# Sliding-window attention and an ELU feed-forward layer: two phases rewritten as one stream with a written-out order

## The chip, the cores and the metric

The kernel runs on one core of one Trainium2 chip. A core has a matrix engine (PE, with its weight loads listed apart as PEld), a vector engine (DVE), an activation engine (ACT), a general-purpose engine (POOL) that also issues transfers, and a sync engine (SP) that only issues transfers; 16 DMA engines move the data. Each engine works through its own list of instructions in order and waits on semaphores. The metric is the device time of one execution in microseconds (us). The kernel before takes 479.98 us, the median of two runs (479.75 to 480.21).

## The reference

Queries, keys and values are [8 batches, 8 heads, 576 positions, 64], all in 32-bit floats. Every query sees the keys at most 32 positions away. The attention output, brought to 4608 tokens by 512, goes through a feed-forward layer (FFN) of width 2048 with an ELU between its two products.

```python
scores = scale * np.matmul(q, k.transpose(0, 1, 3, 2))
mask = np.abs(pos[:, None] - pos[None, :]) <= window      # window = 32
scores = np.where(mask, scores, -1000000000.0)
attn = softmax(scores)
x = (attn @ v).transpose(0, 2, 1, 3).reshape(4608, 512)
h = x @ w_in                                              # 512 -> 2048
g = np.where(h > 0.0, h, np.exp(np.minimum(h, 0.0)) - 1.0)
out = g @ w_out                                           # 2048 -> 512
```

## The kernel before

The program has three stages, one behind the other.

**Attention**, by batch and in it by query block of 64 positions (nine per batch). POOL loads q and k (line 133) and v (lines 167 to 175) from 32-bit to 16-bit on the way, in rows of 64 elements; v is loaded twice, in two tiles shifted by 32 and 96 rows, so that every 128-row key window begins at a tile's row 0. PE turns q and k over, five 128x128 transposes for two heads at a time (line 148), and DVE and ACT take turns in copying the result out (lines 152, 154). For a query block PE makes scores for eight heads against a window of 128 keys (line 188, a contraction of 64), ACT takes the exponential (line 197), DVE multiplies by the 0/1 mask (line 200), and PE makes per head one product with v (line 209) and one with a column of ones (line 212), which is the softmax's denominator. ACT copies the product out (line 218), DVE takes the reciprocal (line 222) and scales (line 225) into `x_st`. There are 72 query blocks.

**Turning x over**: 36 chunks of 128 tokens, four transposes each (line 237), copied by DVE (line 240) and ACT (line 242) in turn.

**FFN**: 18 tiles of 256 tokens. Each has four groups of four 128-wide slices of the hidden layer: 16 matmuls of 256 columns into `psH` (line 263), one exponential over 1024 elements (line 269), two DVE steps for the ELU (`f_sb`, line 271, and `g_sb`, line 273), then eight matmuls of 512 columns into `psY` (line 278). After four groups ACT copies `psY` out (line 285) and SP stores it.

The program is written in this order; a scheduler decides, by dependence and by free buffers, where each instruction stands on its engine, so attention of the next batch is drawn between that of this one. Loads of the two weights (lines 228, 230) stand on POOL behind all loads of q, k and v. The pools of the attention stage are closed before the FFN's are opened, and the FFN's first matmul reads `xT` after the turning-over stage:

```python
    with tc.tile_pool(name="attn_stg", bufs=2) as spool, \
    ...
    with tc.tile_pool(name="xtr_ps", bufs=4, space=bass.MemoryType.PSUM) as xps_pool:
    ...
    with tc.tile_pool(name="moe_sb", bufs=3) as mpool, \
```

## Time and profile before

| what | value |
|---|---|
| time, median of two runs | 479.98 us |
| span of the profiled execution | 479.4 us |
| attention, from its first score matmul to the first transpose of x | 18.4 to 188.1 us |
| turning x over | 188.1 to 200.4 us |
| FFN, first to last matmul | 200.4 to 474.3 us |
| busy share PE / DVE / ACT / POOL | 84% / 53% / 42% / 28% |

The profiled execution is one run; its span, from the first to the last instruction, is 0.6 us below the median time, so what is worked out against the span is compared with the time by adding that. A matmul's duration in the profile holds its way through the array: consecutive ones overlap, so the pace is read from a run of them (the last start to the first, over their number), not from the mean. "Idle before" is the time that the engine waited just before a group, and what ended it. PEclk is the clock that was granted to TensorE as a share of full speed.

### The profile page before, as it was taken

The page shows a single profiled execution, that of the slowest core. Times are in us where ns is not written, and L with a number is a line of the kernel's source. Part 1 is how long each engine was busy: PE and PEld are TensorE (multiplying, and loading weights), DVE is VectorE, ACT ScalarE, POOL GpSimd, SP SyncE. Part 2 cuts the span into 40 slices and gives each one's busy share as a digit, 9 for nine tenths or more (in the row PEclk, how much of TensorE's full clock was granted, in tenths as well). Part 3 has the DMA queues.
Part 4 walks back from the last instruction along what each step waited for, and adds up shares of the span by engine and source line. Part 5 has one row for each costly group of instructions (what it writes and reads, how often), then busy time and mean ns, then how long its engine had stood idle before and what let it go on. Part 6 is the DMA issues. An engine that isn't in the chain of part 4 may idle for free.

```text
span 479.4 us, 9261 instructions
## 1 busy us (share of the span) xinstructions
PE 402.1 (84%) x3889; PEld 282.6 (59%) x3920; DVE 252.2 (53%) x474; ACT 203.5 (42%) x285; POOL 135.8 (28%) x227
## 2 busy tenths in 40 slices
PE   1676877777687876999999999999999999999994
PEld 0465766656575756856565565656656565665652
DVE  0364757567574756564554635445364554635443
ACT  1364656556574655723242333423334143332422
POOL 9999989979777000000000000000000000000000
PEclk9999999999555555999999999999999999999998
DMA  9999999999999990001110111101111011100111
GB/s 61 121 134 152 129 117 153 132 103 153 88 142 92 207 165 1 2 1 44 45 45 0 46 44 45 45 0 45 44 46 40 5 45 44 45 22 24 45 44 44
DMA packets 157033, 33.10 MB, mean 69 GB/s; under 512 B 149824, under 2 KB 151872, under 8 KB 156992
## 3 DMA queue, kind: packets, MB, share of 16 engines
q0 software_dynamic: 152096, 23.08, 70.0%
q1 hardware_dynamic: 4896, 9.44, 5.1%
q8 instruction: 30, 0.49, 0.5%
q14 instruction: 11, 0.09, 0.1%
HBM read 46.14 MB, written 9.44 MB: 116 GB/s over the span
## 4 chain that ended last, share of the span: by engine, by line
PE 46%; DVE 24%; ACT 16%; issue 7%; POOL 3%; DMA 2%; DVEq 0%; ACTq 0%; POOLq 0%
PE psY L278 28%; DVE g_sb L273 9%; ACT e_sb L269 8%; DVE x_st L225 7%; DVE f_sb L271 5%; PE psO L209 5%; PE pt L148 5%; PE psS L212 4%; ACT tT L154 3%; ACT pu L197 2%; PE psH L263 2%; PE psS L188 2%; DVE pm L200 2%; DMA vt<-in_v_dram 2%; ACT xT L242 1%
## 5 line engine op out<-in xcount | busy, mean ns | idle before, releaser
L278 PE MATMUL psY<-w_out_sb,g_sb 128*128 128x512 bf16 x545 | 134.5, 380 | 15.8 <-DVE g_sb L273 14.0
L263 PE MATMUL psH<-xT,w_in_sb 128*128 128x256 bf16 x1152 | 137.4, 273 | 0.7 <-ACT xT L242 0.7
L263 PEld LDWEIGHTS <-w_in_sb 128*128 128x128 bf16 x1152 | 112.7, 98 | 25.0 <-issue 0.8
L269 ACT ACTIVATE e_sb<-psH 128x1024 f32<-128x1024 f32 x72 | 73.8, 1026 | 108.5 <-PE psH L263 95.5
L271 DVE TENSOR_SCALAR f_sb<-e_sb 128x1024 bf16<-128x1024 f32 x72 | 49.5, 688 | 130.3 <-ACT e_sb L269 130.3
L278 PEld LDWEIGHTS <-g_sb 128*128 128x128 bf16 x576 | 50.4, 98 | 86.1 <-DVE g_sb L273 35.1
L273 DVE SCALAR_TENSOR_TENSOR g_sb<-psH,f_sb 128x1024 bf16<-128x1024 f32 x72 | 88.2, 1224 | 7.5
L209 PE MATMUL psO<-vt,pm 128*64 128x64 bf16 x576 | 48.3, 241 | 18.6 <-DVE pm L200 17.2
L209 PEld LDWEIGHTS <-pm 128*64 128x64 bf16 x576 | 41.2, 152 | 25.8 <-DVE pm L200 20.8
L212 PE MATMUL psS<-ones_col,pm 128*64 128x1 bf16 x576 | 45.7, 193 | 9.4 <-ACT pu L197 6.3
L218 ACT COPY oc<-psO 64x512 f32<-64x512 f32 x72 | 41.7, 580 | 27.2 <-PE psS L212 19.0
L197 ACT ACTIVATE pu<-psS 128x512 bf16<-128x512 f32 x72 | 39.5, 594 | 29.3 <-PE psS L188 29.1
L225 DVE TENSOR_TENSOR x_st<-oc,rc_t 64x512 bf16<-64x512 f32 x72 | 49.4, 686 | 4.1 <-ACT oc L218 1.5
L285 ACT COPY y_sb<-psY 128x1024 f32<-128x1024 f32 x18 | 18.2, 1012 | 76.1 <-PE psY L278 76.1
L212 PEld LDWEIGHTS <-pm 128*64 128x64 bf16 x576 | 42.7, 153 | 11.8 <-DVE pm L200 11.8
L200 DVE TENSOR_TENSOR pm<-pu,masks 128x512 bf16<-128x512 bf16 x72 | 29.1, 422 | 31.1 <-ACT pu L197 21.1
L133 POOL DMA_DIRECT2D k_ph<-in_k_dram x40 | 33.9, 868 | 7.2 <-DMA vt<-in_v_dram 6.7
L133 POOL DMA_DIRECT2D q_ph<-in_q_dram x40 | 34.1, 872 | 0.1
L154 ACT COPY tT<-pt 128x640 bf16<-128x640 bf16 x32 | 22.2, 693 | 27.7 <-PE pt L148 27.2
L148 PE MATMUL pt<-ident,q_ph 128*128 128x128 bf16 x160 | 24.7, 300 | 10.7 <-DMA q_ph<-in_q_dram 9.7
L148 PE MATMUL pt<-ident,k_ph 128*128 128x128 bf16 x160 | 21.5, 307 | 13.3 <-ACT tT L154 8.9
L169 POOL DMA_DIRECT2D vt<-in_v_dram x16 | 30.6, 1915 | 0.3 <-issue 0.3
(33 smaller groups left out, 190.4 us busy)
## 6 DMA issues: line engine op xcount, KB each, us to landing
out_dram<-y_sb SPq DMA_DIRECT2D x18, 512.0 KB, 2.8
vt<-in_v_dram POOLq DMA_DIRECT2D x16, 560.0 KB, 8.5
q_ph<-in_q_dram POOLq DMA_DIRECT2D x32, 128.0 KB, 7.4
k_ph<-in_k_dram POOLq DMA_DIRECT2D x32, 128.0 KB, 5.7
w_in_sb<-in_moe_w_in_dram POOLq DMA_DIRECT2D x1, 2048.0 KB, 16.2
w_out_sb<-in_moe_w_out_dram POOLq DMA_DIRECT2D x1, 2048.0 KB, 25.6
q_ph<-in_q_dram POOLq DMA_DIRECT2D x8, 64.0 KB, 7.3
k_ph<-in_k_dram POOLq DMA_DIRECT2D x8, 64.0 KB, 4.5
```

The costliest lines, as they stand in the source:

```text
L133: nc.gpsimd.dma_start(out=dst[0:np_, so, :, :], in_=src_hbm[b, :, lo:hi, :].rearrange("h p d -> p h d"))
L148: nc.tensor.transpose(pt[:, so, :], src[:, so, 2 * hp:2 * hp + 2, :], ident)
L197: nc.scalar.activation(pu, psS_hq, AX.Exp, scale=SCALE)
L209: nc.tensor.matmul(psO[bq:bq + QB, h, :], lhsT=pm[:, h, :], rhs=vt[:, c, :], start=True, stop=True)
L212: nc.tensor.matmul(psS[bq:bq + QB, h % 2, (h // 2) * QB:(h // 2) * QB + 1], lhsT=pm[:, h, :], rhs=ones_col, start=True, stop=True)
L218: nc.scalar.copy(oc[bq:bq + QB], psO[bq:bq + QB])
L225: nc.vector.tensor_mul(x_st[bq:bq + QB, chk, :], oc[bq:bq + QB], rcb)
L263: nc.tensor.matmul(psH[:, j, :], lhsT=w_in_sb[:, do, fo * 128:(fo + 1) * 128], rhs=xT[:, do, tok0:tok0 + TT], start=(do == 0), stop=(do == ...
L269: nc.scalar.activation(e_sb, psH, AX.Exp)
L271: nc.vector.tensor_scalar(f_sb, e_sb, -1.0, 0.0, ALU.add, ALU.min)
L273: nc.vector.scalar_tensor_tensor(g_sb, psH, 0.0, f_sb, ALU.max, ALU.add)
L278: nc.tensor.matmul(psY[:, ts, :], lhsT=g_sb[:, j, ts * 128:(ts + 1) * 128], rhs=w_out_sb[:, fo, :], start=(fg == 0 and j == 0), stop=(fg = ...
```

## The change

The three stages become one program whose instructions are put on the engines in the order in which they are written (`tc.manual_schedule()`).

Attention is cut into pieces for a pair of query blocks (36 pairs of 128 tokens): `QK` (16 score matmuls) with `SM` (one exponential over 1024 elements), `MK` (two mask multiplies of 512 elements) with `AV` for heads 0 to 3, `AV` for heads 4 to 7, and `X` (four transposes and a copy by DVE). The masked weights lie in a tile with 64 zero columns behind each block's 64 (`pm`, three times 64 wide per head), so that the two blocks' products with v, each with 128 weight columns, add up in one PSUM tile of 128 tokens; v has a 65th column of ones, so the denominator comes with the product (eight matmuls of 65 columns for four heads). `T` turns over q or k for two heads: six transposes of 96 columns and a copy by ACT. The FFN tile is 512 tokens: `Hm` is four matmuls of 512 columns and an exponential over 512 elements, `Hv` the two DVE steps, `Y` four matmuls of 512 columns.

q and k are loaded by SP without a change of type, in rows of 384 elements that lie together in memory; the cast to 16 bit is done on the chip, for batch 0 by DVE and ACT, for the others by POOL. v is loaded once, for the even query blocks; the odd blocks' windows are copied from those within the on-chip memory by SP (`shift_v`). The weights are loaded in eight parts by POOL, behind v of batch 0 and ahead of v of batch 1.

Work of pairs is divided into steps; step i holds `QK` and `SM` of pair i, `MK` and `AV` of pair i-1, `X` of pair i-2. Steps 0 to 5 are emitted before the first `Hm`. After that FFN tile t gives 16 slots of `Hm` for tile t and, from the second tile on, 16 of `Y` for tile t-1, and the remaining attention pieces are laid between the slots. `Hv` of a slot is emitted behind the next slot. PSUM holds one buffer each for scores (two banks), attention output, transposes and `Y`, and three for `Hm`.

```diff
+    def load_qk(b, half, eng):
+        for nm, src in (("q", q), ("k", k)):
+            t = stg.tile([PR, HP, TPP * D], FP32, tag="stg")
+            eng.dma_start(
+                out=t, in_=src[b, half * HP:(half + 1) * HP].rearrange(
+                    "h (p t) d -> p h (t d)", t=TPP))
...
+    def load_v(b):
+        vt = vw[b % NVB]
+        vb = v[b].rearrange("h s d -> s h d")
+        nc.gpsimd.dma_start(out=vt[WIN:128, 0, :, 0:D], in_=vb[0:128 - WIN])
+        for qb in range(2, NQB - 1, 2):
+            lo = qb * QB - WIN
+            nc.gpsimd.dma_start(out=vt[:, qb, :, 0:D], in_=vb[lo:lo + 128])
...
+    def shift_v(b):
+        vt = vw[b % NVB]
+        nc.sync.dma_start(out=vt[0:QB, 1:NQB:2], in_=vt[QB:128, 0:NQB - 1:2])
+        nc.sync.dma_start(out=vt[QB:128, 1:NQB:2], in_=vt[0:QB, 2:NQB:2])
+
+    def T(b, nm, hp):
+        src = stage[nm, b]
+        pt = psT_p.tile([128, TPP, PR], BF16, tag="psT")
+        for j in range(TPP):
+            nc.tensor.transpose(pt[:, j, :], src[:, j, 2 * hp:2 * hp + 2, :],
+                                ident[0:PR, 0:PR])
...
+        nc.scalar.copy(dst.rearrange("c (p t) -> c t p", t=TPP), pt)
...
+    def QK(i):
+        psS = psS_p.tile([128, 2, 2, HP, QB], FP32, tag="psS")
+        for s in range(2):
...
+                nc.tensor.matmul(
+                    psS[:, h % 2, s, hp, :],
...
+    def SM(i):
...
+        nc.scalar.activation(pu, psS, AX.Exp, scale=SCALE)
...
+    def MK(i):
...
+            nc.vector.tensor_mul(dst, pu[:, :, s], mb)
+
+    def AV(i, g):
...
+                nc.tensor.matmul(
+                    o[:, j, :], lhsT=p[:, h, s * QB:s * QB + 128],
+                    rhs=vw[b % NVB][:, qb, h, :],
+                    start=(s == 0), stop=(s == 1))
+        rc = xsp.tile([128, HP], FP32, tag="rc")
+        nc.vector.reciprocal(rc, o[:, :, D])
+        rb = _bap(rc, [rc.ap[0], rc.ap[1], [0, D]])
+        nc.vector.tensor_mul(live["X", i][:, g * HP:(g + 1) * HP, :],
+                             o[:, :, 0:D], rb)
...
+    def Hm(t, fo):
...
+        ps = psH_p.tile([128, TT], FP32, tag="psH")
+        for do in range(NDO):
+            nc.tensor.matmul(ps, lhsT=w_in_sb[:, do, fo * 128:(fo + 1) * 128],
+                             rhs=xts[t][:, do, :],
+                             start=(do == 0), stop=(do == NDO - 1))
+        e = ep.tile([128, TT], FP32, tag="e")
+        nc.scalar.activation(e, ps, AX.Exp)
+        es[t, fo] = (ps, e)
+
+    def Hv(t, fo):
+        ps, e = es.pop((t, fo))
+        f = ep.tile([128, TT], BF16, tag="f")
+        nc.vector.tensor_scalar(f, e, -1.0, 0.0, ALU.add, ALU.min)
+        nc.vector.tensor_tensor(gs[t][:, fo, :], ps, f, ALU.max)
...
+        for b in range(1, B):
+            need = (b * NQB) // 2
+            extra[max(0, need - 6)].append(
+                lambda b=b: (load_v(b), load_qk(b, 0, nc.sync),
+                             load_qk(b, 1, nc.sync)))
+            extra[max(0, need - 5)].append(
+                lambda b=b: (cast(b, "q", (nc.gpsimd, nc.gpsimd)),
+                             cast(b, "k", (nc.gpsimd, nc.gpsimd)),
+                             shift_v(b)))
+            for hp in range(HP):
+                extra[need - 4 + hp].append(lambda b=b, hp=hp: T(b, "q", hp))
+                extra[need - 4 + hp].append(lambda b=b, hp=hp: T(b, "k", hp))
...
+            for n, (f, a, s) in enumerate(slots):
+                f(a, s)
+                if waiting is not None:
+                    Hv(*waiting)
+                    waiting = None
+                if f is Hm:
+                    waiting = (a, s)
+                want = base + (goal - base) * (n + 1) // max(1, len(slots) - 2)
+                while pos < min(want, goal):
+                    rest[pos][1]()
+                    pos += 1
```

How this moves instructions is shown at two places. The first is DVE. In the kernel before, in the middle of the attention stage, DVE's list holds attention only (`pm` is the mask multiply, `rc_t` the reciprocal, `x_st` the scaled output, `tT` a copy of turned-over q or k):

```order
L225 TENSOR_TENSOR x_st_86<-oc_1628,rc_t_1630 64x512
L225 TENSOR_TENSOR x_st_86<-oc_1663,rc_t_1665 64x512
L200 TENSOR_TENSOR pm_1679<-pu_1677,masks_75 128x512
L200 TENSOR_TENSOR pm_1714<-pu_1712,masks_75 128x512
L152 COPY tT_1787<-pt_1789 128x640
L222 RECIPROCAL rc_t_1700<-psS_1668 64x8
L222 RECIPROCAL rc_t_1735<-psS_1703 64x8
L225 TENSOR_TENSOR x_st_86<-oc_1698,rc_t_1700 64x512
```

Every mask multiply there stands behind other attention work. In the changed kernel, in the third FFN tile, the same engine's list is this (`f` and `g` are the two steps of `Hv`, `pm0` the masked weights, `o` the product with v, `xt` the turned-over x):

```order
L216 TENSOR_SCALAR f_2043<-e_2028 128x512
L217 TENSOR_TENSOR g_1605<-ps_2023,f_2043 128x512
L165 TENSOR_TENSOR pm0_108<-pu_1870,masks_98 128x2x4x64 x2
L181 RECIPROCAL rc_2058<-o_2049 128x4
L183 TENSOR_TENSOR xs_2048<-o_2049,rc_2058 128x256
L216 TENSOR_SCALAR f_2080<-e_2066 128x512
L217 TENSOR_TENSOR g_1605<-ps_2061,f_2080 128x512
L181 RECIPROCAL rc_2092<-o_2083 128x4
L183 TENSOR_TENSOR xs_2048<-o_2083,rc_2092 128x256
L216 TENSOR_SCALAR f_2114<-e_2100 128x512
L217 TENSOR_TENSOR g_1605<-ps_2095,f_2114 128x512
L197 COPY xt_1718<-pt_2117 128x4x128
```

The two mask multiplies now stand behind `f` and `g` of an `Hm` slot, and `f` waits for that slot's exponential.

The second place is POOL. In the kernel before its list ends with the last batch's v and the two weights:

```order
L167 DMA vt_3110<-in_v_dram 96x64
L169 DMA vt_3110<-in_v_dram 128x35x64
L175 DMA vt_3110<-in_v_dram 32x64
L162 MEMSET vt_3118 32x64 x3
L165 MEMSET vt_3118 32x64
L167 DMA vt_3118<-in_v_dram 32x64
L169 DMA vt_3118<-in_v_dram 128x35x64
L175 DMA vt_3118<-in_v_dram 96x64
L228 DMA w_in_sb_80<-in_moe_w_in_dram 128x4x2048
L230 DMA w_out_sb_81<-in_moe_w_out_dram 128x16x512
```

In the changed kernel the weights stand near the front of POOL's list, between v of batch 0 (`vw0`) and v of batch 1 (`vw1`), and the casts of batch 1's q (`t_267`) and k (`t_270`) follow:

```order
L109 DMA vw0_105<-in_v_dram 96x8x64
L112 DMA vw0_105<-in_v_dram 128x8x64 x3
L114 DMA vw0_105<-in_v_dram 96x8x64
L276 DMA w_in_sb_99<-in_moe_w_in_dram 128x4x512 x4
L280 DMA w_out_sb_100<-in_moe_w_out_dram 128x4x512 x4
L109 DMA vw1_106<-in_v_dram 96x8x64
L112 DMA vw1_106<-in_v_dram 128x8x64 x3
L114 DMA vw1_106<-in_v_dram 96x8x64
L103 CAST t_267<-t_259 96x4x6x64
L103 CAST t_267<-t_263 96x4x6x64
L103 CAST t_270<-t_261 96x4x6x64
L103 CAST t_270<-t_265 96x4x6x64
```

The weights moved from the end of the list to near its front, and casts, which POOL did not have before but for the mask, came in. On SP, which before issued only the 18 stores, `shift_v` of batch 0 now stands ahead of the loads of batch 1's q and k, and waits for v of batch 0 to land.

More of the change, by code (lines that the diff above doesn't have):

```diff
@@ L13 @@
 ALU = mybir.AluOpType
+PSUM = bass.MemoryType.PSUM
 def _bap(ap, new_ap):
@@ L53 @@
     N_TOK = B * S
-    D_MODEL = H * D
+    DM = H * D
     D_FF = moe_w_in.shape[1]
@@ new lines @@
+    psH_p = ctx.enter_context(tc.tile_pool(name="psH", bufs=3, space=PSUM))
+    psY_p = ctx.enter_context(tc.tile_pool(name="psY", bufs=1, space=PSUM))
+    ident = const.tile([128, 128], BF16)
+    masks = const.tile([128, 3, QB], BF16)
+    w_in_sb = const.tile([128, NDO, D_FF], BF16)
+    w_out_sb = const.tile([128, NFO, DM], BF16)
+    NKB = 2
+    NVB = 3
+    NPB = 2
+    kT = [const.tile([128, HP, KW], BF16, name=f"kT{i}") for i in range(NKB)]
+    qT = [const.tile([128, HP, S], BF16, name=f"qT{i}") for i in range(NKB)]
@@ new lines, in cast @@
+    def cast(b, nm, engs):
+        t = bfp.tile([PR, TPP, H, D], BF16, tag="bf")
+        for half in range(2):
+            src = stage.pop((nm, b, half)).rearrange(
+                "p h (t d) -> p h t d", t=TPP)
+            dst = t[:, :, half * HP:(half + 1) * HP, :].rearrange(
+                "p t h d -> p h t d")
+            e = engs[half]
+            if e is nc.scalar:
+                nc.scalar.copy(dst, src)
+            else:
+                e.tensor_copy(dst, src)
+        stage[nm, b] = t
```

385 lines of the change are left out of this document (169 added, 216 removed).

## The prediction

> **What bounds the kernel now.** I read the page's busy shares and slices first, then the windows by stage, then the chain and the timeline inside the FFN.
>
> ```profile
> PE 402.1 (84%) x3889; PEld 282.6 (59%) x3920; DVE 252.2 (53%) x474; ACT 203.5 (42%) x285; POOL 135.8 (28%) x227
> PEclk9999999999555555999999999999999999999998
> ...
> 18.40:188.10 169.70, 126.34 (x2009) 104.95 (x2009) 106.61 (x292) 99.72 (x173) 118.57 (x186) 0.80 1.86 130
> 188.10:200.40 12.30, 11.64 (x144) 11.03 (x144) 8.33 (x19) 10.16 (x19) 0.00 (x0) 0.78 0.00 1
> 200.40:474.30 273.90, 257.97 (x1697) 163.04 (x1727) 134.69 (x144) 89.30 (x89) 0.00 (x0) 1.00 0.09 33
> ```
>
> The window rows give, behind the length, busy time of PE, PEld, DVE, ACT and POOL, then the granted clock. There are two different limits. The FFN takes 273.9 us at clock 1.00 with PE busy 94%. Attention takes 169.7 us with no engine busy more than 74%: scores, exponential, mask and product wait for each other in turn. PE's 84% is thus a mean of a full stage and one that holds many short matmuls. What the FFN must cost on PE:
>
> ```profile
> 300.45 3.22 PE L263 MATMUL psH<-xT,w_in_sb 128*128 128x256 bf16 x28
> 300.87 1.02 ACT L269 ACTIVATE e_sb<-psH 128x1024 f32<-128x1024 f32 x1 [4.82 <-PE psH L263]
> 301.92 0.69 DVE L271 TENSOR_SCALAR f_sb<-e_sb 128x1024 bf16<-128x1024 f32 x1 [3.27 <-ACT e_sb L269]
> 302.72 1.23 DVE L273 SCALAR_TENSOR_TENSOR g_sb<-psH,f_sb 128x1024 bf16<-128x1024 f32 x1
> 304.00 1.90 PE L278 MATMUL psY<-w_out_sb,g_sb 128*128 128x512 bf16 x8 [0.33 <-DVE g_sb L273]
> L278 PE MATMUL psY<-w_out_sb,g_sb 128*128 128x512 bf16 x545 | 134.5, 380 | 15.8 <-DVE g_sb L273 14.0
> ```
>
> Eight 512-column matmuls take 1.90 us of which the last's own length is 0.38: seven starts in 1.52, 0.217 us each. The whole FFN is 1152 times that (half of it now cut in 256s), 250 us; 24 of the 273.9 are waits. So most of what can go is the 200 us before the FFN, if its PE work fits beside 250 us of FFN.
>
> **The PE work of the change.** The big matmuls stay at 1152 x 0.217 = 250 us. The small ones:
>
> ```profile
> 61.69 1.23 PE L148 MATMUL pt<-ident,k_ph 128*128 128x128 bf16 x10 [0.94 <-DVE tT L152]
> 66.09 0.77 PE L188 MATMUL psS<-tT 64*128 64x64 bf16 x16
> L188 PE MATMUL psS<-tT 64*128 64x64 bf16 x576 | 26.4, 235 | 3.3 <-ACT tT L154 2.8 <-DVE rc_t L222 0.5
> L148 PE MATMUL pt<-ident,q_ph 128*128 128x128 bf16 x160 | 24.7, 300 | 10.7 <-DMA q_ph<-in_q_dram 9.7
> 193.46 6.93 ACT L242 COPY xT<-psXT 128x512 bf16<-128x512 bf16 x13 [0.27 <-PE psXT L237]
> 196.00:197.00 1.00, 1.00 (x19) 0.79 (x3) 1.00 (x3) 1.00 0.00 0
> ```
>
> Scores: 16 in 0.77, less 0.24 of the last, over fifteen, so 0.036 each and 0.58 per pair. A transpose with 128 weight columns in the attention stage: 10 in 1.23, less 0.30 of the last, over nine, gives 0.103. At granted clock 1.00 (the fourth number behind the window's length in the last row), from 193.46 on, ACT makes 13 copies in 6.93 us without a pause, each with its neighbour on DVE standing for eight transposes: 0.067 each, and there ACT sets the pace, so PE needs no more. The new stream runs like the FFN, at clock 1.00, so I take 0.060 for every matmul with 128 weight columns (`AV` 576, `T` 384, `X` 144), with 0.052 (half of 0.103, the pace following the clock) and 0.103 as ends. The Trainium skill, "TensorE: Matmul & The Clock Gate", section LDWEIGHTS, gives a weight load as its columns over 1.2 GHz, 107 ns for 128; by that the sum would be some 42 us longer. The warm stretch above speaks against it: 67 ns.
>
> Of these, 18 `T`, 6 `QK`, ten half `AV` and 4 `X` are done before the first `Hm`. What is left after it: 900 x 0.060 = 54, 480 scores x 0.036 = 17, big 250: **321 us** (314 to 360). Gone are the second product with ones (576), the second shifted v and 72 copies on ACT (line 218).
>
> **Until the first `Hm`.**
>
> ```profile
> q1 hardware_dynamic: 4896, 9.44, 5.1%
> out_dram<-y_sb SPq DMA_DIRECT2D x18, 512.0 KB, 2.8
> 168.00:172.00 4.00, 1.95 (x26) 1.43 (x25) 1.55 (x4) 2.35 (x4) 0.00 (x0) 0.50 1.24 208
> 3.70 1.00 POOL L133 DMA_DIRECT2D q_ph<-in_q_dram  x1
> 7.25 0.13 PEld L148 LDWEIGHTS <-q_ph 128*128 128x128 bf16 x2 [7.25 <-DMA q_ph<-in_q_dram]
> L133 POOL DMA_DIRECT2D k_ph<-in_k_dram x40 | 33.9, 868 | 7.2 <-DMA vt<-in_v_dram 6.7
> L93 POOL CAST masks<-mask_f 128x192 bf16<-128x192 f32 x1 | 0.4, 361 | 0.0
> L77 POOL MEMSET mask_f<- 128x192 f32 x1 | 0.3, 259 | 0.0
> L128 POOL MEMSET q_ph<- 64x512 bf16 x8 | 4.2, 524 | 0.3
> L154 ACT COPY tT<-pt 128x640 bf16<-128x640 bf16 x32 | 22.2, 693 | 27.7 <-PE pt L148 27.2
> L197 ACT ACTIVATE pu<-psS 128x512 bf16<-128x512 f32 x72 | 39.5, 594 | 29.3 <-PE psS L188 29.1
> L200 DVE TENSOR_TENSOR pm<-pu,masks 128x512 bf16<-128x512 bf16 x72 | 29.1, 422 | 31.1 <-ACT pu L197 21.1
> L222 DVE RECIPROCAL rc_t<-psS 64x8 f32<-64x8 f32 x72 | 14.8, 205 | 23.1 <-PE psS L212 22.6
> L225 DVE TENSOR_TENSOR x_st<-oc,rc_t 64x512 bf16<-64x512 f32 x72 | 49.4, 686 | 4.1 <-ACT oc L218 1.5
> L240 DVE COPY xT<-psXT 128x512 bf16<-128x512 bf16 x18 | 7.6, 424 | 3.1 <-PE psXT L237 2.0
> ```
>
> SP's stores moved 9.44 MB in 5.1% of 16 engines' 479.4 us, 24.4 us, so 386 GB/s while they ran. Batch 0's q and k, 2.36 MB in 32 bits, need 6.1 us; with 2.8 to land and the casts (1536 elements, by L269's 1.02 us for 1024 about 1.5 on ACT, two in a row) they are ready at 13. Eight `T` then follow one by one, as one transpose buffer must be emptied by ACT each time: PE 0.62 and 0.2 for the last one's way out, the copy 576/640 of 693 ns, hand-overs 0.1: 1.5 each, done at 25.
>
> Batch 1 is later. POOL starts its first load at 3.70; five loads of v at 868 ns bring it to 8, and v lands about 4 later (3.6 us pass from the first issue at 3.70 to the first transpose at 7.25). Only then does SP, held by `shift_v`, issue batch 1's q and k, at 12.5. They share the engines with the weights, 4.2 MB at the 208 GB/s of the last stretch in which only weights move, 20 us; at half their rate they take 12 and are all in at 26. POOL's casts of 1536 elements: the two memsets, 259 ns for 192 elements and 524 for 512, give 0.83 ns an element, so 361 + 1344 x 0.83 = 1.5 us; in proportion to the 192-element cast it would be 2.9. I take 2.2, and with two casts done before the last load is in, the fourth ends at 31. Step 0's second `T` needs it. Five steps follow; a step there goes round DVE and the one output buffer: product's end 0.2, reciprocal 0.2, hand-over 0.1, scaling 0.44 (256 elements, between 205 and 686 ns), `X` copy 0.42, two masks 0.84 (L200), eight `AV` matmuls at the cold 0.103 = 0.82, scaling again 0.8, and `AV` 0.82, 0.2 of hand-overs: 4.9. So 31 + 24.5, and two `T` of batch 2 at its end: **57 us** (46 if batch 1's data come as soon as batch 0's turn is over; 68 if the weights hold up v of batch 1 and a cast takes 2.9).
>
> **Waits of PE in the stream.** Order decides: PE's `AV` needs both masks, which on DVE stand behind `f` and `g` of a slot. From the last big matmul's start slot: 0.16 way out and 0.04, exponential 0.59 (L197, same size), 0.03, `f` 0.42 (half of L271's 0.69, plus the fixed part), 0.11, `g` 0.60 (512 elements as L225, 0.69, the next op starting 0.09 before its end), masks 2 x 0.42, 0.05: 2.84 us. `AV`'s eight matmuls end seven starts later, 2.84 + 0.42, where without a wait they would end 0.48 after arrival; so the wait is 2.78 less the PE work between that `Hm` and `AV`. In the order of the 27 pairs from the second tile on, this is `T Y` ten times (1.23, wait 1.55), `Y` six times (0.87, wait 1.91), `QK Y` once (1.33), `Y T Hm` twice (0.68), `QK Y Hm` three times (0.46), `QK Y T Hm` four times (0.10), `Y Hm` once (1.04): 33 us. In the first tile, without `Y`, DVE is the longer: 16 x (0.42 + 0.11 + 0.60) + 4 x 2.74 (a pair's masks 0.84, two reciprocals with scalings 1.48, `X` copy 0.42) = 29 us against PE's 24, and it waits some 0.7 for each first product: 8 us. The last tile's `Y` run alone, and three times the one `Y` buffer must be copied out (0.85): 3; the second half of a pair waits for its buffer now and then: 1. Together **45 us** (25 if slots overlap better; 75).
>
> **The casts against DVE.** Four casts of 2.2 per batch fall into the stream for six batches. The trace has no POOL compute beside DVE but memsets, under which L200 stays at 422 ns, so the bounds are nothing and all of 24 x 2.2 = 53 us. I take one mask multiply per batch held for half a cast: **7 us**. The Trainium skill, "SBUF — State Buffer", section "SBUF: two separate sides", says that a DVE instruction in a two-port mode or with two inputs in SBUF and a POOL instruction that reads SBUF exclude each other, the later one fully blocked; no run here shows it. If each cast held PE for its whole length by that, the sum would be 482.
>
> **Sum.** After the last `Y`: way out 0.2, copy 0.6, then as before 4.0 from the copy's end to the span's:
>
> ```profile
> 474.33 1.01 ACT L285 COPY y_sb<-psY 128x1024 f32<-128x1024 f32 x1 [4.23 <-PE psY L278]
> ```
>
> (475.34 to 479.4.) 57 + 321 + 45 + 7 + 5 = 435 us of span, and 0.6 between span and median: **436 us**, 9% less. ACT (144 x 0.59 + 36 x 1.03 + 64 x 0.62 + 36 x 0.59 = 183) and DVE (144 x 1.13 + 36 x 2.74 = 261) stay below that. The transfers of a batch, 2.36 MB at 386 GB/s and 0.59 MB of v at the 130 GB/s of the attention row, take 11 of the 48 us that 4.5 steps last; stores that queue on SP behind `shift_v` and behind loads have three buffers and one store in 10 us.
>
> **Rivals.**
> 1. *POOL comes late, slower than before.* `T` of the last-cast half of k follows its load by two steps, about 21 us at 10.6 a step; load 8 and four casts must fit in 22. Up to 3.4 us a cast nothing is late. At 5.8 (twice 2.9, by waiting for DVE) each of six batches stops PE for 9, and the start grows by 14: 504. From 5.2 on it passes the time before. For it: POOL's price is known from 192 elements only; against: 0.83 ns per element.
> 2. *The casts hold DVE.* Each of the 24 keeps `f` or a mask waiting for half its length to all of it, and PE with them: 26 to 53 us in place of 7, so 455 to 482. For it: both then read the same memory at once; against: PE may run three `Hm` ahead of DVE, 5 us, so a late `f` alone costs nothing.
> 3. *The small matmuls keep the cold pace.* For: attention ran at 0.103 also where the clock is given as 1.00; against: the 13 copies. 900 x 0.043 = 39 more: 475.
> 4. *A longer start*: v of batch 1 waits for all weights, 20 us, and steps wait for it: 452.
> 5. *Few waits*: the masks are mostly in time: 435 - 33 - 7, about 396.
>
> **Chances.** Forecast 0.58, longer start 0.10, few waits 0.08, cold pace 0.08 (spread around 475, half under 470), casts that hold DVE 0.08 (half under 470), POOL late 0.08. A change of 2% (470.4 to 489.6) is what a measurement here tells from none. Faster 0.84, same 0.08, slower 0.08. The terms' ends together give 390 to 560, but they won't all fall on one side: 404 to 458 for the forecast itself, and 402 to 474 leaves out most of rivals 5 and 1 and the far ends of 2 and 3, under 0.2.
>
> **What would show it.** First `Hm` near 57 us, with `T` before it waiting for a POOL cast; `AV` groups led by an idle of 1.5 us ended by the mask multiply, some 30 us in all; transposes in the stream at 0.06 per start with granted clock 1.00; `T` never waiting for POOL after the first tile. It is wrong if the clock falls in the stream, if the casts last over 3.4 us, or if the big matmuls start further apart than 0.217.

## The result, and the profile after

The changed kernel takes 453.31 us (451.61 and 455.0) against 479.98: a ratio of 0.945, with a 95% interval of 0.936 to 0.954. It is faster by 5.5%, not by the 9% of the forecast; the profiled execution's span is 449.9 us against the 435 of the sum. (Of the runs below, one of e5_serial took 661.95 us at a granted clock of 0.80; its times are those of its three other runs.) Two lines of the page, then the windows by stage (length, busy time of PE, PEld, DVE, ACT and POOL, granted clock, DMA share, GB/s):

```profile
PE 337.4 (75%) x2784; PEld 173.8 (39%) x2832; DVE 261.9 (58%) x557; ACT 268.3 (60%) x283; POOL 84.9 (19%) x92
...
PEclk9999999999989999969999999999899999999999
```

```profile
0.00:78.40 78.40, 22.42 (x300) 17.98 (x301) 22.24 (x51) 46.72 (x27) 36.19 (x51) 1.00 1.54 207
...
112.00:382.00 270.00, 230.94 (x1933) 115.66 (x1968) 180.51 (x385) 172.03 (x194) 36.97 (x31) 0.97 0.36 75
382.00:429.00 47.00, 45.84 (x243) 21.31 (x246) 32.62 (x66) 19.37 (x33) 0.00 (x0) 1.00 0.09 34
```

The first `Hm` starts at 78.4 us instead of the forecast 57. PE's share fell from 84% to 75%, and the kernel is faster all the same: PE has less to do (337 us in place of 402). Where attention runs beside the FFN, from 112 to 382 us, PE idles 39 of 270 us and the mean clock is 0.97; without attention, from 382 on, it idles 1 of 47.

What PE and its weight loads waited for from the first `Hm` on (sum in us, times, longest):

```profile
PEld L176 <- DVE pm L165: 53.9, 62, 3.4
PE o L176 <- DVE pm L165: 33.2, 25, 2.9
...
PE pt L195 <- ACT kT L131: 6.0, 10, 1.3
...
PE pt L125 <- ACT qT L131: 1.6, 3, 0.6
```

The waits for the mask product (`pm`, line 165) lead by far. They show twice: on PE's matmuls after the idle of the array, 33.2 us, and on the weight load ahead of them, 53.9, part of which lies under matmuls that still run. The time that they cost should lie between.

The groups of instructions that came out otherwise than priced (busy us, mean ns of one):

```profile
L131 ACT COPY kT<-pt 128x576 bf16<-128x576 bf16 x32 | 66.7, 2084 | 12.0 <-PE pt L125 11.5
L103 POOL CAST t<-t 96x1536 bf16<-96x1536 f32 x28 | 41.8, 1522 | 130.8 <-DMA t<-in_q_dram 130.6 <-DMA t<-in_k_dram 0.2
L216 DVE TENSOR_SCALAR f<-e 128x512 bf16<-128x512 f32 x144 | 71.3, 495 | 78.2 <-ACT e L210 78.0
L165 DVE TENSOR_TENSOR pm<-pu,masks 128x512 bf16<-128x512 bf16 x72 | 34.7, 523 | 29.0 <-ACT pu L153 29.0
```

ACT's copy of the transposed q or k lasts 2.08 us, not the 0.62 taken from the kernel before; there are 64 such copies. The POOL cast lasts 1.52 us, not 2.2. `f` and the mask take 495 and 523 ns on the mean where the forecast had 420 for each.

One stretch shows how these meet. First PE, then DVE and POOL at the same place, then the window row of what follows:

```profile
187.61 1.03 PE L227 MATMUL psY<-w_out_sb,g 128*128 128x512 bf16 x4
191.51 0.23 PE L176 MATMUL o<-vw,pm 128*128 128x65 bf16 x1 [2.87 <-DVE pm L165]
193.11 0.57 PE L176 MATMUL o<-vw,pm 128*128 128x65 bf16 x7 [1.37 <-DVE pm L165]
193.49 1.90 PE L206 MATMUL ps<-xt,w_in_sb 128*128 128x512 bf16 x4
...
203.80 1.04 PE L206 MATMUL ps<-xt,w_in_sb 128*128 128x512 bf16 x4
204.67 0.42 PE L125 MATMUL pt<-ident,t 96*128 96x96 bf16 x6
204.93 1.03 PE L227 MATMUL psY<-w_out_sb,g 128*128 128x512 bf16 x4
```

```profile
188.28 1.58 DVE L216 TENSOR_SCALAR f<-e 128x512 bf16<-128x512 f32 x1 [1.11 <-ACT e L210]
...
190.50 2.56 DVE L165 TENSOR_TENSOR pm<-pu,masks 128x512 bf16<-128x512 bf16 x2
...
188.11 4.67 POOL L103 CAST t<-t 96x1536 bf16<-96x1536 f32 x3 [3.79 <-DMA t<-in_q_dram]
...
191.30:198.10 6.80, 5.22 (x31) 2.76 (x32) 3.53 (x7) 2.58 (x2) 3.97 (x4) 0.50 0.93 76
```

While POOL casts, `f` lasts 1.58 us and two masks 2.56, and `AV` waits twice, 4.2 us in all. Then the granted clock is 0.50 for 6.8 us: four matmuls of `Hm` take 1.90 us where they take 1.04 at full clock. So a long wait is paid twice, as idle time and as slow matmuls behind it.

### The profile page after: what moved, and what is told of

Read it like the earlier page. It is cut to its first block, busy times and chain, and to the rows that moved or that the text cites. A ratio compares the mean times of both kernels' runs of the same rounds, so it can differ in the third digit from the quotient of the medians.

```text
span 449.9 us, 7032 instructions
## 1 busy us (share of the span) xinstructions
PE 337.4 (75%) x2784; PEld 173.8 (39%) x2832; DVE 261.9 (58%) x557; ACT 268.3 (60%) x283; POOL 84.9 (19%) x92
## 4 chain that ended last, share of the span: by engine, by line
PE 49%; DVE 17%; ACT 13%; DMA 13%; issue 6%; POOL 1%; SPq 0%; ACTq 0%; POOLq 0%
PE ps L206 20%; PE psY L227 20%; DMA vw<-in_v_dram 6%; DVE g L217 6%; ACT kT L131 5%; DVE f L216 5%; DVE pm L165 5%; DMA w_out_sb<-in_moe_w_out_dram 5%; ACT e L210 5%; PE o L176 4%; DMA t<-in_q_dram 2%; PE pt L125 2%; PE pt L195 2%; ACT qT L131 2%; ACT pu L153 1%
## 5 line engine op out<-in xcount | busy, mean ns | idle before, releaser
L210 ACT ACTIVATE e<-ps 128x512 f32<-128x512 f32 x144 | 92.1, 640 | 113.4 <-PE ps L206 105.6
L206 PE MATMUL ps<-xt,w_in_sb 128*128 128x512 bf16 x549 | 148.6, 389 | 2.8 <-DVE xt L197 1.3
L227 PE MATMUL psY<-w_out_sb,g 128*128 128x512 bf16 x555 | 144.7, 382 | 5.6 <-ACT y L232 3.6
L216 DVE TENSOR_SCALAR f<-e 128x512 bf16<-128x512 f32 x144 | 71.3, 495 | 78.2 <-ACT e L210 78.0
L217 DVE TENSOR_TENSOR g<-ps,f 128x512 bf16<-128x512 f32 x144 | 99.6, 692 | 5.4
L227 PEld LDWEIGHTS <-g 128*128 128x128 bf16 x576 | 52.8, 99 | 58.8 <-issue 6.7
L131 ACT COPY kT<-pt 128x576 bf16<-128x576 bf16 x32 | 66.7, 2084 | 12.0 <-PE pt L125 11.5
L206 PEld LDWEIGHTS <-w_in_sb 128*128 128x128 bf16 x576 | 51.4, 99 | 49.8 <-issue 5.2
L131 ACT COPY qT<-pt 128x576 bf16<-128x576 bf16 x32 | 66.6, 2082 | 5.0 <-PE pt L125 4.7
L103 POOL CAST t<-t 96x1536 bf16<-96x1536 f32 x28 | 41.8, 1522 | 130.8 <-DMA t<-in_q_dram 130.6
L125 PEld LDWEIGHTS <-t 96*128 96x128 bf16 x384 | 26.9, 110 | 63.6 <-issue 35.3
```

What stands on the lines that cost most here:

```text
L103: e.tensor_copy(dst, src)
L125: nc.tensor.transpose(pt[:, j, :], src[:, j, 2 * hp:2 * hp + 2, :], ident[0:PR, 0:PR])
L131: nc.scalar.copy(dst.rearrange("c (p t) -> c t p", t=TPP), pt)
L206: nc.tensor.matmul(ps, lhsT=w_in_sb[:, do, fo * 128:(fo + 1) * 128], rhs=xts[t][:, do, :], start=(do == 0), stop=(do == NDO - 1))
L210: nc.scalar.activation(e, ps, AX.Exp)
L216: nc.vector.tensor_scalar(f, e, -1.0, 0.0, ALU.add, ALU.min)
```

## The experiments

All times are medians; each ratio is to the kernel before, run beside it. The table takes five readings from one profile of each kernel: the start of the first `Hm`, the rest of the span after it, in that rest the waits of `AV`'s weight load for masks, the time at half clock (granted clock over windows of 1 us, up to 4 us before the end), and the cold time. This last is the stretch from the first `Hm` to the trace's first record of the clock: the rows read 1.00 there, but the matmuls run at the half pace (in e1_copy four matmuls of `Hm` take 1.90 us at 84.79, and three take 0.81 at 87.60). Runs of one kernel differ by up to 5.7 us (e1_copy, 438.55 to 444.29), so differences of a few us between two profiles show little.

| kernel | us | ratio, interval | first Hm | rest | mask waits | half clock | cold |
|---|---|---|---|---|---|---|---|
| after | 453.3 | 0.945, 0.936 to 0.954 | 78.4 | 371.5 | 53.9 | 17.1 | 3.6 |
| e1_copy | 441.7 | 0.922, 0.917 to 0.927 | 78.1 | 361.2 | 55.2 | 10.2 | 9.2 |
| e2_order | 466.0 | 0.973, 0.969 to 0.977 | 77.4 | 388.6 | 58.1 | 30.7 | 4.2 |
| e3_dmacast | 439.8 | 0.919, 0.915 to 0.923 | 77.6 | 360.2 | 47.4 | 3.4 | 6.0 |
| e4_mkearly | 414.6 | 0.868, 0.863 to 0.873 | 79.2 | 333.7 | 3.5 | 0 | 4.8 |
| e5_serial | 536.5 | 1.118, 1.114 to 1.122 | 275.8 | 260.5 | - | 0 | 4.3 |
| e6_order2 | 456.4 | 0.951, 0.947 to 0.954 | 77.1 | 376.5 | 54.8 | 23.9 | 8.9 |
| e7_copy_order | 432.4 | 0.901, 0.897 to 0.905 | 63.6 | 365.6 | 50.7 | 23.9 | 5.6 |
| e8_all | 384.8 | 0.802, 0.799 to 0.804 | 61.6 | 322.4 | 9.6 | 6.8 | 3.2 |
| e9_act | 424.9 | 0.884, 0.879 to 0.889 | 87.2 | 332.3 | 8.1 | 10.2 | 4.1 |
| e10_dve | 420.2 | 0.874, 0.871 to 0.877 | 90.5 | 329.4 | 4.0 | 6.8 | 4.9 |
| e11_mix | 410.7 | 0.855, 0.853 to 0.857 | 89.5 | 320.0 | 4.9 | 0 | 3.8 |
| e12_mix | 380.1 | 0.792, 0.789 to 0.794 | 58.6 | 320.0 | 4.3 | 3.4 | 5.4 |

In e9_act to e11_mix some products read another batch's v (see there). The questions were four: what holds the start, what the slow copies cost, what the casts on POOL cost, and what the place of the mask product costs. The start first. The chain of waits of after, cut to its steps:

```profile
15.99 21.35 DMA w_out_sb<-in_moe_w_out_dram
...
37.63 16.70 DMA vw<-in_v_dram
...
54.35 0.60 SPq L119
...
55.04 10.86 DMA t<-in_q_dram
...
73.00 1.48 POOL t L103
...
74.52 0.68 PE pt L125 x6
```

v of batch 1 waits for the weights on POOL's queue; SP's copy within `vw` (line 119, `shift_v`) waits for that v; batch 2's q stands behind it on SP; then come the casts and `T`. Theory A is that this chain sets the start; rival B, that the 16 slow copies do.

### e1_copy: the copy writes contiguously

```diff
-        nc.scalar.copy(dst.rearrange("c (p t) -> c t p", t=TPP), pt)
+        nc.scalar.copy(dst.rearrange("c (p t) -> c p t", t=TPP),
+                       pt.rearrange("c t p -> c p t"))
```

> Changes one thing: ACT's copy of the transposed q and k (line 131) reads PSUM with a step and writes SBUF contiguously; after, it was the other way round, 2.08 us a copy against 0.69 for the 640-element copy of the kernel before. The same values are computed. Theory A (the start waits for the order of the transfers: v of batch 1 behind the weights, the second shift of v on SP ahead of batch 2's q and k; the slow copies matter in the stream only): the copy falls to 0.6 to 0.8 us; the first Hm stays between 72 and 78 us (it was 78.4; only the four or so copies at the very end of the start come off); in the stream the waits for the mask products fall from 53.9 to some 40, since no 2.1 us copy stands ahead of an exponential any more; time 436 to 446. Rival B (the copies set the start): first Hm at 55 to 62, time 420 to 432. Rival C (a step of this size costs ACT the same wherever it stands): copy still about 2.1 us, time as after, 449 to 457.

The same group in the profile of this kernel:

```profile
L131 ACT COPY kT<-pt 128x576 bf16<-128x576 bf16 x32 | 20.3, 636 | 21.0 <-PE pt L125 21.0
```

2084 ns became 636, for the same 576 elements: the writes of 2 bytes at a distance of 12 had cost 1.45 us, the stepped read from PSUM costs next to nothing (the 693 ns for 640 elements of before would be 624 for 576). The first `Hm` did not move (78.1), which speaks for A. One step of A fell, though: the mask waits did not shrink (53.9 to 55.2). Most of the 10.3 us that the rest gained are elsewhere: `X`'s 6.0 and `T`'s 1.6 us of waiting for these copies, which hold the one buffer for transposes, are gone. Half clock fell by 6.9 us, but the cold stretch grew by 5.6, so the clock gives 0.6 at most. Some 2 us stay unexplained, less than this kernel's runs differ by.

### e2_order and e6_order2: the transfers of the start earlier

```diff
+        load_v(1)
         FC = 512
         w_in_v = moe_w_in.rearrange("(o p) f -> p o f", p=128)
...
-        shift_v(0)
         cast(0, "q", (nc.vector, nc.scalar))
         cast(0, "k", (nc.vector, nc.scalar))
+        load_qk(1, 0, nc.sync)
+        load_qk(1, 1, nc.sync)
+        shift_v(0)
```

In both, `shift_v` of batch 1 goes behind the loads of batch 2. Of the later batches it is a piece of its own in e2_order, one step later than in after; in e6_order2 it stands in the piece that loads the next batch, behind those loads.

> Changes only the order of transfers in the start: v of batch 1 is loaded ahead of the weights on POOL's queue, the q and k loads of batch 1 ahead of the first shift of v on SP, and those of batch 2 ahead of the second shift. The copies stay at 2.08 us. Theory A (transfers set the start): v of batch 1 is in by 33 instead of 54 us, SP comes free, batch 2's q and k are there some 15 us earlier, and the first Hm falls from 78.4 to 60 to 70 us; nothing changes after it; time 436 to 445. Rival B (the copies of T set the start): first Hm stays at 75 or later, time within 2% of 453.

> The same early transfers as in e2_order, but no piece of work is added to the list that is dealt out between the big matmuls, so that PE's instructions stand in exactly the order of after (in e2_order the shift of v had become a piece of its own, which moved 356 PE instructions to other slots). Theory A' (two chains of nearly equal length set the start: the transfers, 78.4, and eight plus eight copies of 2.08 us with what follows, 77.4; e2_order's 13 us were lost in the stream by the moved pieces and the longer waits for masks): first Hm at 76 to 78, the stream as in after, time 447 to 456. Rival (the later shift of v or the other queue order costs the time in the stream): 460 or more.

In both the first `Hm` stayed, at 77.4 and 77.1 us. The chain of waits of e2_order now runs through the copies:

```profile
17.73 2.07 ACT kT L131
...
19.85 0.65 PE pt L125 x6
...
55.19 6.46 DVE pm L165 x2
```

A copy, then transposes, then the next copy: eight copies follow each other so before the first step, and more in the steps for batch 1. One row is of another kind: two mask products take 6.46 us instead of 0.8, beside POOL's casts of batch 1 (6.37 in the chain of e6_order2), so this chain is not made of copies alone. So A as first put, that the transfers alone set the start, fell, and so did B; A', two chains that end within 1 us of each other, is what the single edits leave. e2_order's 466 us were not expected. e6_order2, with PE's instructions in exactly the order of after, took 456.4, a little over the top of its range and below the 460 of the rival. Its rest is 12.1 us shorter than that of e2_order: the extra pieces had moved some 350 matmuls to other slots, which made waits of 58.1 + 9.7 + 3.8 us (masks, `X`, `T`) from 54.8 + 5.5 + 1.4. Half clock and cold time together differ by 2.1 us (34.9 and 32.8), and PE waits for no `shift_v` in the rest of either. The order of pieces is thus worth some 10 us by itself. Against after, e6_order2's rest is 5.0 us longer with the waits alike; 12.1 us more of it run at half pace.

### e7_copy_order: both together

> e1_copy and e6_order2 together; PE's order is that of after. Theory A' (two chains of nearly equal length): with both shortened the first Hm falls to 58 to 66 us although neither edit alone moved it; the rest as in e1_copy (361 us from the first Hm to the end), time 418 to 430. Rival (a third chain stands behind, POOL's casts of batch 1 after the eight issues of weights, or the weights themselves): first Hm at 70 or later, time 432 to 442.

The first `Hm` came at 63.6 us: neither edit alone had moved it by more than 1.3, both together moved it by 14.8. This settles A'. The time, 432.4, is 2 us over the range and just inside that of the rival, as the rest was 365.6 and not 361; the rival's first `Hm`, at 70 or later, did not come. Batch 2's casts now fall into the first tile; DVE and POOL there:

```profile
75.22 6.14 DVE L217 TENSOR_SCALAR f<-e 128x512 bf16<-128x512 f32 x1
...
75.39 5.69 POOL L103 CAST t<-t 96x1536 bf16<-96x1536 f32 x4
```

One `f` of 0.42 us lasted 6.14, until the four casts were over (its record starts 0.17 us ahead of theirs). `Hm` waited 5.1 us for the `g` behind it, and two units of half clock follow, from 79.4 us on. In all, half clock and cold time are 29.5 us, where e1_copy has 19.5.

### e3_dmacast: no POOL casts in the stream

```diff
+    def load_cast(b):
+        for nm, src in (("q", q), ("k", k)):
+            t = bfp.tile([PR, TPP, H, D], BF16, tag="bf")
+            sv = src[b].rearrange("h (p t) d -> t p h d", t=TPP)
+            for j in range(TPP):
+                nc.gpsimd.dma_start(out=t[:, j], in_=sv[j])
+            stage[nm, b] = t
...
```

Batches 2 to 7 use it in place of the loads by SP and the casts by POOL.

> Takes the POOL casts out of the stream: q and k of batches 2 to 7 are loaded by POOL's queue in 256-byte pieces that the transfer casts to 16 bit, straight into the tile that T reads, as the kernel before did; batch 1 and the start keep the loads and casts of after. Theory D (a POOL cast keeps DVE out while it runs): f (line 216) returns from a mean of 495 ns to about 427 and the mask product (line 165) from 523 to about 416, no DVE instruction over 1 us is left in the stream, DVE's busy time falls by some 15 us; as the lost time lay in 24 short bursts, some of them off PE's path, the time falls by 4 to 12 us, to 441 to 449. Rival (the long DVE instructions come from something else, such as the loads writing SBUF): they stay, and the time stays within 1%. A second rival: the small pieces come late, T waits for the transfer, and the time rises over 460.

All lengths of `f`, after and then here (shortest, median, longest ns, first and last start):

```profile
L216 DVE TENSOR_SCALAR f<-e x144: 415/427/1702, 81.0 to 428.6; 128x512 bf16<-128x512 f32 x144
```

```profile
L224 DVE TENSOR_SCALAR f<-e x144: 416/427/806, 80.1 to 416.5; 128x512 bf16<-128x512 f32 x144
```

Only a remainder of up to 806 ns is left, and the kernel is faster by 13.5 us (439.8, 1 us below the range of D): the rest fell by 11.3. Mask waits fell by 6.5 us, and half clock and cold time together by 11.3, worth 5.6 at most. By this one pair of profiles the casts had cost about as much through the clock as through the waits; of the four spells of half clock in after, the two that begin at 191.3 and 290.3 us, 10.2 us long together, begin at the end of a group of casts. The 256-byte pieces that replaced the contiguous loads came in time.

### e4_mkearly: the mask product one to two slots earlier

```diff
-                st.append(lambda i=i: (QK(i), SM(i)))
+                st.append(lambda i=i: (MK(i - 1) if i else None, QK(i), SM(i)))
             if 1 <= i <= NPAIR:
-                st.append(lambda i=i: (MK(i - 1), AV(i - 1, 0)))
+                st.append(lambda i=i: (MK(i - 1) if i == NPAIR else None,
+                                       AV(i - 1, 0)))
```

> Changes only where the mask product of a pair stands: on DVE at the next pair's QK piece, one or two slots earlier, instead of directly ahead of the product of weights and v that needs it. Theory E (PE waits because the masks stand on DVE behind f and g of the last slot: 33 us of waits were forecast by this, 53.9 seen): PE's waits for the mask product fall from 53.9 to under 20 us in sum, time 415 to 430. Rival F (the exponential itself comes late, as ACT is held by 2.1 us copies and by the queue of Hm exponentials; DVE then waits in order for it and f and g come late too): the waits move to Hm (psH buffers) or stay; time 440 to 455.

414.6 us, at the foot of theory E's range. The waits from the first `Hm` on:

```profile
PE pt L125 <- ACT qT L131: 9.4, 15, 1.8
PE pt L195 <- ACT kT L131: 5.5, 10, 1.1
...
PE o L176 <- DVE xs L183: 3.6, 6, 1.3
PE o L176 <- DVE pm L165: 1.9, 2, 1.4
```

33.2 us became 1.9 on PE's row and 53.9 became 3.5 on the weight load's, and there was no half clock between the cold stretch and the last `Y`. The rest of the span fell by 37.8 us. At most 8.0 of them are the clock (20.7 us at half pace became 4.8); 7.8 came back as `T` waiting for the slow copies, as PE now reaches them sooner. That leaves some 38 us for the masks themselves, between the two ways of counting, or a little more, as `AV` now also waits 3.6 us for the scaling ahead of it (`xs`).

### e5_serial: attention first, then the FFN

> Undoes the interleaving alone: all attention pieces first, in the same order, with nine tiles of transposed x held, then the whole FFN. Operations, copies, casts and loads are those of after. Theory (laying the two beside each other is what gains): attention alone is bound by ACT, per pair 1.0 us of exponential and 1.8 copies of 2.08, 4.7 us, or 36 pairs in 170 to 200 us, then the FFN at PE's pace, 250 to 262 us: 425 to 465 us, the clock full in the FFN and much of the attention at the lower clock. If the time is under 445, the interleaving of after, with its waits for masks and the clock lost by them, gains nothing over running one after the other; if it is over 465 it gains what was forecast or more. Rival (attention alone is as slow as in the kernel before, 190 us or more): 455 to 470.

536.5 us, far over all ranges, and 83 us more than the change as made. The FFN alone took 260.5 us to the end of the span, but attention alone 275.8. A stretch of 100 us of it and the waits of the whole kernel:

```profile
150.00:250.00 100.00, 48.09 (x673) 38.16 (x673) 39.99 (x98) 67.18 (x42) 18.08 (x16) 1.00 0.36 50
```

```profile
PE pt L123 <- ACT qT L129: 58.6, 27, 9.8
PE pt L193 <- ACT kT L129: 43.1, 26, 1.7
```

ACT is busy 67% and PE 48%: `T`, copy, `X`, scores and exponential go round one buffer each, every piece in turn, with nothing to fill the gaps. The 1.00 in the row is no full clock: it lies before the first record, and six `T` take 0.64 us there (201.96), not 0.42. PE waits another 17.7 us for masks; four mask products last over 4 us, beside casts. I had counted ACT's busy time as the length. So this attention, in this order, is slower alone than that of the kernel before, and the interleaving is what makes it cheap: 78.4 + 371.5 in place of 275.8 + 260.5.

### e8_all: copy, transfers and early masks

> e7_copy_order and e4_mkearly together: contiguous writing of the transposed q and k, transfers of the start reordered, mask products early. If the parts add: first Hm at 58 to 66 us as in e7_copy_order, the rest as in e4_mkearly (334 us) less 2 to 6 for the short copies, the clock full from the first Hm on: 388 to 402. If the early masks already took what the short copies gain in the stream: 396 to 404. If the start does not shorten: 408 to 415.

384.8 us, under the range: first `Hm` 61.6 as hoped, the rest 322.4, shorter than the 328 to 332 worked out: the copies' waits that e4_mkearly still had (9.4 and 5.5) are gone too. One hole is left, at batch 2's casts, on POOL, DVE and PE:

```profile
74.29 5.69 POOL L103 CAST t<-t 96x1536 bf16<-96x1536 f32 x4
...
74.76 5.50 DVE L217 TENSOR_SCALAR f<-e 128x512 bf16<-128x512 f32 x1
...
81.37 0.90 PE L177 MATMUL o<-vw,pm 128*128 128x65 bf16 x8 [5.53 <-DVE pm L166]
82.09 1.90 PE L207 MATMUL ps<-xt,w_in_sb 128*128 128x512 bf16 x4
```

Cast, held `f`, a wait of 5.53 us, and matmuls at half pace: the same chain as in after.

### e9_act to e12_mix: the casts on other engines

```diff
-                lambda b=b: (cast(b, "q", (nc.gpsimd, nc.gpsimd)),
-                             cast(b, "k", (nc.gpsimd, nc.gpsimd)),
+                lambda b=b: (cast(b, "q", (nc.vector, nc.scalar)),
+                             cast(b, "k", (nc.vector, nc.scalar)),
```

(e11_mix and e12_mix; all on ACT in e9_act, all on DVE in e10_dve. The loads of q and k move up behind the casts of the batch before.)

> e8_all with all casts of batches 1 to 7 on ACT in place of POOL, and each batch's loads issued as soon as the casts of the batch before have freed the buffers; PE's order is that of e8_all. Theory D (casts on POOL keep DVE out, in e8_all once for 5.5 us with a PE wait of 5.5 and some 7 us at half clock behind it, and some 8 us of the start wait for the casts): no DVE instruction over 1 us, no PE wait over 2 us after the first Hm, first Hm at 52 to 60, ACT busy 181 + 28 x 1.47 = 222 us, time 364 to 374. Rival (ACT's casts of 1.5 us stand ahead of exponentials, masks come late again): PE waits for masks of 10 us and more, time 378 to 390.

> The same with the casts on DVE, 28 x 1.1 us more there less the 15 us that POOL held: DVE some 269 of some 370 us. Theory D: time 364 to 376, a little over e9_act if DVE, which has f, g and the masks, is the tighter engine. Rival (DVE now bounds the stream, Hm waits for g): 378 or more.

> The same with half of the casts on DVE and half on ACT (first halves of the heads on DVE, second on ACT). Theory D: as the better of the two others or up to 3 us below it, 362 to 373, since the casts of batch 1 then run two at a time in the start. If either engine is the bound, between the two.

In these three the load of v of a batch moved up too, ahead of the last `AV` that reads the buffer it fills; those products read another batch's v, and PE stood some 33 us in the start until it was in. Their times miss the forecast ranges for that reason (the 420.2 of e10_dve lies in its rival's open range, 378 or more, which says nothing here), and only their rests can be read: 332.3 on ACT, 329.4 on DVE, 320.0 shared. Of these, 2.8, 1.3 and 0.3 us are still waits for that v. Other waits remain, as the two rivals had it, but not the ones that they named: with all casts on ACT, PE waits 4.7 us for masks, 3.7 for a copy of q and 6.2 for copies of `Y`; with all on DVE 5.7 for the scaling and 8.4 for `X`'s copies, but 0.2 for `g`; shared, none of these is over 2.7. The rival of e9_act had named 10 us of masks, that of e10_dve waits for `g`.

> e8_all with the casts of batches 1 to 7 shared between DVE (first halves of the heads) and ACT (second halves), and each batch's q and k loads issued as soon as those casts have freed the buffers; v is loaded where e8_all loads it (in e9_act, e10_dve and e11_mix the load of v had been moved with the others, ahead of the last products that read the buffer it fills, so that their output is not the reference's and PE stood 33 us in the start). PE's order is that of e8_all. Theory D (casts on POOL held DVE, once for 5.5 us with a half clock behind it, and came late in the start): no DVE instruction over 1.2 us, clock full from the first Hm on, first Hm at 53 to 60, the rest 316 to 321 us as in e11_mix: 369 to 381, below e8_all. Rival (casts on DVE and ACT cost the stream as much as the lock did): 382 to 390, as e8_all.

With v loaded where it was: 380.1 us, first `Hm` at 58.6, rest 320.0. `f` and `pm` here, in the view of all their lengths:

```profile
L217 DVE TENSOR_SCALAR f<-e x144: 408/426/811, 61.2 to 357.3; 128x512 bf16<-128x512 f32 x144
L166 DVE TENSOR_TENSOR pm<-pu,masks x72: 414/417/425, 27.2 to 320.5; 128x512 bf16<-128x512 bf16 x72
```

No DVE instruction is held by a cast any more, and the intervals of e8_all and e12_mix are apart (0.799 to 0.804, 0.789 to 0.794): 1.2%, in line with the 3.0 us of the start and 2.4 of the rest. Theory D holds, one point of it not quite: one window of 3.4 us at half clock is left, beside the 5.4 cold us. This is the best version found, 21% below the kernel before and 16% below the change as made.

## Why the prediction was right or wrong

The forecast of 436 was 17 us low, the sign and the range (402 to 474) held. That the sum came so near is partly luck: its errors have both signs, 21 us too little for the start, 27 too much for PE's work, 22 too little for the waits and the casts. By one of its own signs it was wrong: the clock did fall in the stream.

1. **The start, 57 us: wrong by 21.** Two steps failed. "Eight `T` then follow one by one ... 1.5 each" rested on the copy's price from elements alone; the write's step made it 2.08 us, and `T` followed `T` at 2.8. And the sum had no term for v of batch 1, which waited for all the weights: it was in at 54 us. The range of the start, 46 to 68, allowed for that at its upper end and was still too narrow. Rival 4 named the mechanism, with a price of 452; it is what the chain shows, but e2_order and e6_order2 say that it was only half of the cause, and that 452 is so near to 453 rests on the errors of PE's work and the waits, which nearly cancel.
2. **PE's work, 321 us: too high by 27, and below the range of 314 to 360.** The big matmuls were right: 1.04 us for four, less 0.38 of the last, is 0.22 each over three. The small ones went faster still than the 0.060: the six `T` that start at 204.67 give way to `Y` after 0.26 us, 0.043 each. `AV` and the scores show it too:

```profile
203.46 0.41 PE L141 MATMUL psS<-qT,kT 64*128 64x64 bf16 x16
...
209.59 0.41 PE L176 MATMUL o<-vw,pm 128*128 128x65 bf16 x8
209.83 1.02 PE L206 MATMUL ps<-xt,w_in_sb 128*128 128x512 bf16 x4
211.56 0.39 PE L195 MATMUL pt<-ident,xs 128*128 128x128 bf16 x4
211.78 0.59 PE L206 MATMUL ps<-xt,w_in_sb 128*128 128x512 bf16 x2
```

   Eight `AV` in 0.24 is 0.030 each, sixteen scores in 0.34 (to 203.80) 0.021, four `X` in 0.22 0.055. 496 x 0.030 + 276 x 0.043 + 128 x 0.055 + 480 x 0.021 = 44 us against 71. Rival 3 is refuted and the 0.052 taken as the lower end, half of the 0.103, was none.
3. **Waits, 45 us, and casts, 7: too low by 22.** 371.5 - 250 - 44 - 4 of tail leaves 74. The largest term, masks at 33 us, was right in cause and nearly in size: e4_mkearly makes it some 38, part of it, by e3_dmacast, for masks that casts held. What the sum lacked are `T` and `X` waiting for the slow copies (7.6), and the clock: 17.1 us at half of it and 3.6 cold ones cost up to 10.3. "The new stream runs like the FFN, at clock 1.00" is the sentence that failed. Some 18 of the 74 us are not broken down here.
4. **The casts.** 1.52 us instead of 2.2, so rival 1 (from 3.4 us a cast on) did not come, yet dearer than the 7: e3_dmacast gains 11.3 us in the rest, up to 5.6 of them by the clock. The rule that the prediction cites for rival 2 (the Trainium skill, "SBUF — State Buffer", section "SBUF: two separate sides"), that DVE and POOL exclude each other at the on-chip memory, has its runs now: in e8_all 0.42 us of `f` became 5.50 beside four casts that took 5.69 together. It takes in only some of DVE's work. In after 14 `f` and 5 masks overlap a cast, and 12 and 5 of them are longer for it; 21 others that overlap one read the matmul results in PSUM and keep their lengths, `g` among them:

```profile
L217 DVE TENSOR_TENSOR g<-ps,f x144: 690/692/693, 81.8 to 429.1; 128x512 bf16<-128x512 f32 x144
```

   In the stream DVE so lost some 12 us, but most casts meet no such instruction or one that is not late, and the rival's 455 to 482 did not come.
5. **Rival 5**, few waits at 396, did not come either; e4_mkearly, which moves one product in the order of emission, brings the waits for masks to that state (1.9 and 3.5 us), at 414.6 with the longer start. **ACT**, which I summed to 183 us, was busy 268, for which the 64 copies, 1.46 us longer each, more than account (93 us); since it is not the bound, this cost 10 us in the stream and, with the transfers, 15 in the start.

## What to carry to other kernels

When a stage is filled by laying two streams beside each other, look at what each piece needs from the other engines and emit that one or two slots ahead: here the place of one DVE product was worth more (39 us) than the whole change (27). Take the price of a copy from a row with the same step in its write, not from its element count. If one edit to a start does not move it, ask for a second chain of the same length before giving up the theory: two edits worth 0.3 and 1.3 us alone were worth 14.8 together.

## What the hardware showed that was not expected

- **Half clock comes in units.** From the first record of the clock on, the time at half clock is a multiple of 3.41 us in every kernel: 17.1 is five, 10.2 three, 30.7 nine, 23.9 seven, 6.8 two. In after the longest spell, two units, follows the longest wait (187.61 to 193.49 above). The Trainium skill, "TensorE: Matmul & The Clock Gate", section "Part 1: The HAM clock gate (the "warmup" mystery)", gives half rate after an idle window of about 3.4 us, with windows that run freely; the trace agrees with the length, while here the windows were not wholly idle: in the 3.4 us before the half clock of 191.3 the matmuls of `Y` ran until 188.64. That the phase of these windows also makes the spread of after's two runs (451.6 and 455.0) is only argued.
- **The clock shown in the start is not the pace.** Before the trace's first record of the clock (82 us in after, 118 in the kernel before) the rows give 1.00, but six `T` take 0.64 us there and 0.42 in the stream (204.67). So the 1.00 beside slow transposes, which rival 3 counted for itself, was no full clock:

```profile
17.96 0.64 PE L125 MATMUL pt<-ident,t 96*128 96x96 bf16 x6 [9.89 <-ACT qT L131]
```

- **A stepped write of 16-bit values** costs ACT 3.6 ns an element (2084 / 576) instead of 1.1 (636 / 576), a stepped read from PSUM next to nothing. The Trainium skill, "SBUF — State Buffer", section "Door 1: The DMA port swizzle (why `[64,N]` ≈ `[32,N]`)", charges each access that crosses into a new line of 16 bytes; the direction agrees, and the size is measured here.
- **POOL need not compute to hold DVE.** In e12_mix POOL has no casts in the stream, and eight `f` of over 0.6 us each start while POOL issues a load of v and end some 0.2 us after it:

```profile
121.32 0.77 DVE L217 TENSOR_SCALAR f<-e 128x512 bf16<-128x512 f32 x1
...
120.99 0.87 POOL L112 DMA_DIRECT2D vw<-in_v_dram  x1 [7.68 <-PE o L177]
```

  Four masks that start during an issue of POOL there keep their 0.42 us. No run here separates the two further.
